# Five attention rows moved into the last batch, own memory for the raw weights, and the nearest-expert step moved

## The chip, the cores and the metric

The kernel runs on one core of one Trainium2 chip. The metric is the device time of one execution in microseconds. Three runs of the kernel before gave 1133.48, 1134.14 and 1136.73 us, so the median is 1134.14 us.

## What is computed

The reference chains three parts, all in float32:

```
p_packed = sm_attn(p, k, v)              # 8 batches x 8 heads, 32 packed queries over 576 keys
out      = sm_attn(q, p_packed, p_packed) # 576 queries over the 32 packed rows
x        = out as 4608 tokens x 512
x        = moe1(x)   # 8 experts, 576 tokens each; experts are filled in the order of sorted logits
x        = moe2(x)   # 8 experts, the best one per token, weighted by its softmax
expert:    relu(x @ w1[e]) @ w2[e]       # 512 -> 1024 -> 512
```

The first mixture has capacity 576 per expert, so which expert closes first has to be found by a search over all logits before the first expert's tokens are known.

## The kernel before

**Attention** (`attention`, L60) loops over 8 batches. Batch `i` makes the packed attention of batch `i` (`pack_scores`, `pack_exp`, `pack_eT`, `pack_v`, `pack_D`, `pack_T`), the query scores of batch `i-1` (`query`), and the softmax and transposes of batch `i-2` (`sm_aT`, `logits`). What comes out per batch is `aT`, the transposed attention weights. An output row tile, called a row below, is `out_rows(b, c)` (L357): two float32 products on TensorE (L367), one copy out of PSUM on ScalarE (L370), one store to the DRAM tensor `xs` from SyncE's queue (L372). There are 8 x 5 = 40 of them in the list `todo`. `fill(n)` takes the next n of them; `FILL` says how many in each batch at three places, `TAIL` how many between the steps that follow the last batch (5, 3, 2, 0).

**Routing.** While the rows that are left run in `forward`, phase 0 of the router runs between them: `nearest` (the best expert per token, seven VectorE instructions) and `search` (eight rounds; each is a comparison `ge` on VectorE, five small products on TensorE at L654, three VectorE instructions down to `cp`, one product, and three or four VectorE instructions from `cmx` to the next `ge`). The search ends with `code`, and `ex`, the chosen expert. Then the token list `idx` is built, and GpSimd gathers the tokens with five indirect DMAs (L1263, into `G`). `nearest` for the first 20 columns of the logits is already done in the last batch: that call is `early()`, with `EARLY = 20`.

**Experts.** A unit is one expert's 576 tokens (units 0 to 7), then blocks of up to 580 tokens of the second mixture. TensorE does the first layer (L1517) and the second (L1572). Each float32 operand is split into a high and a low part, so each product is three. The weights go through four raw buffers of 0.5 MB: a DMA fills one, ScalarE writes the high half (L1460, `w1H`), VectorE the low half (L1466, `w1L`), and then the buffer is free for the next load (`fetch`). Tokens are turned by TensorE (L1300), split by ScalarE (L1301, `XH`) and VectorE (L1302, `XL`). Later phases of the search run between the products of the units.

**Order of the work.** There is no run-time scheduler: each engine runs its own instructions in the order that was written. `Sched` (L1044) keeps a clock per engine while the program is written, and `S.advance` puts instructions of waiting chains (search, splits, token turns) between the rows and products by estimated costs. What becomes ready earlier in that model is written earlier.

**Memory.** The raw buffers come out of a pool that is opened after `closing()` has given the attention's memory back, so they lie where attention tiles lay. Their first load is issued in `fetch`, called from `gather_next` after all rows are written.

## Time and profile before

| | us |
|---|---|
| median of 3 runs | 1134.14 |
| profiled execution, its time | 1134.52 |
| its span | 1132.8 |
| TensorE busy | 1041.8 (92% of the span) |
| VectorE busy | 713.5 (63%) |
| ScalarE busy | 444.6 (39%) |
| GpSimd busy | 488.7 (43%) |

The span is the stretch between the first and the last instruction; 1.7 us lie around it. In the rows below PE is TensorE, PEld its weight loads, DVE VectorE, ACT ScalarE, POOL GpSimd, SP SyncE. Times are counted from the start of the span. A timeline row gives start and duration, then engine, line, operation, output and inputs, and in brackets how long the engine sat idle before and what ended that.

### The profile page before, as it was taken

To read this page: it belongs to the slowest core of one execution; us is meant where nothing else is said; L and a number is where in the kernel's file an instruction comes from. 1 tells how busy PE (TensorE), PEld (TensorE's weight loads), DVE (VectorE), ACT (ScalarE), POOL (GpSimd) and SP (SyncE) were. 2 spreads that over 40 slices of the span, in tenths; PEclk is the share of its full clock that TensorE was granted. 3 is DMA by queue.
4 is the path that set the end of the run, shared out by engine and by line. 5 is a ranking of instruction groups with operands and counts; after the bars stand their busy time and mean duration, and the time that the engine had idled before them with its cause. 6 is when DMAs were issued, how large, how long until landed. Compare 5 with 4: busy or idle time off the path is not lost.

```text
span 1132.8 us, 24490 instructions
## 1 busy us (share of the span) xinstructions
PE 1041.8 (92%) x9152; PEld 967.9 (85%) x9152; DVE 713.5 (63%) x2105; ACT 444.6 (39%) x940; POOL 488.7 (43%) x595
## 2 busy tenths in 40 slices
PE   6689797699899998999999999989999999999996
PEld 4577664588888897989999999979898999999995
DVE  1468777688979889884556566655555556455430
ACT  4467564323332323333434334333443433434331
POOL 1123301212424224047565344477787778742401
PEclk9899899699999999999999999999999999999998
DMA  9989246633243242224345343554445454433301
GB/s 257 278 228 259 53 168 201 158 75 117 64 139 113 80 137 57 99 89 145 117 134 138 99 145 93 135 143 126 126 144 143 106 170 136 127 125 102 99 20 43
DMA packets 117857, 146.90 MB, mean 130 GB/s; under 512 B 55946, under 2 KB 80522, under 8 KB 116704
## 3 DMA queue, kind: packets, MB, share of 16 engines
q1 hardware_dynamic: 102368, 116.43, 35.9%
q0 software_dynamic: 13776, 28.76, 8.7%
q8 instruction: 74, 1.21, 0.5%
q14 instruction: 55, 0.45, 0.2%
q10 hardware_dynamic: 1584, 0.05, 0.1%
HBM read 116.31 MB, written 29.52 MB: 129 GB/s over the span
## 4 chain that ended last, share of the span: by engine, by line
PE 60%; DVE 12%; issue 9%; DMA 9%; POOL 5%; ACT 2%; SPq 2%; POOLq 0%; ACTq 0%; DVEq 0%
PE mm L1572 26%; PE mm L1517 22%; DMA G<-ys,gi 4%; POOL out_dram L1344 3%; PE sc L170 2%; POOL G L1282 2%; PE tr L367 1%; DMA raw<-in_moe_w_dram 1%; PE sc L367 1%; DVE hL L1494 1%; DMA G<-xs,idx 1%; DMA vm<-in_v_dram 1%; PE tr L150 1%; DVE cmx L1008 1%; PE b L150 1%
## 5 line engine op out<-in xcount | busy, mean ns | idle before, releaser
L1517 PE MATMUL mm<-XH,w1H 128*128 128x290 f32 (+3 forms) x1024 | 306.9, 300 | 8.7 <-ACT XH L1301 3.8
L1517 PE MATMUL mm<-XL,w1H 128*128 128x290 f32 (+3 forms) x1024 | 307.9, 301 | 0.5 <-DVE XL L1321 0.3
L1517 PE MATMUL mm<-XH,w1L 128*128 128x290 f32 (+3 forms) x1024 | 305.4, 298 | 2.8 <-DVE w1L L1466 2.7
L1572 PE MATMUL mm<-hH,w2H 128*128 128x288 f32 (+3 forms) x768 | 231.9, 302 | 1.1 <-ACT YT L1577 1.1
L1572 PE MATMUL mm<-hH,w2L 128*128 128x288 f32 (+3 forms) x768 | 232.7, 303 | 0.0
L1572 PE MATMUL mm<-hL,w2H 128*128 128x288 f32 (+3 forms) x768 | 231.7, 302 | 0.1
L1492 ACT ACTIVATE hH<-mm 128x290 fp32r<-128x290 f32 (+3 forms) x256 | 105.7, 413 | 293.4 <-PE mm L1517 279.6
L1517 PEld LDWEIGHTS mm<-XH,w1H 128*128 128x128 f32 x1024 | 195.2, 191 | 11.2 <-ACT XH L1301 4.2
L1517 PEld LDWEIGHTS mm<-XH,w1L 128*128 128x128 f32 x1024 | 195.4, 191 | 3.9 <-DVE w1L L1466 3.5
L1517 PEld LDWEIGHTS mm<-XL,w1H 128*128 128x128 f32 x1024 | 194.7, 190 | 1.6 <-DVE XL L1321 0.8
L1494 DVE SCALAR_TENSOR_TENSOR hL<-mm,hH 128x290 fp32r<-128x290 f32 (+3 forms) x256 | 115.2, 454 | 116.7 <-ACT hH L1492 115.6
L1282 POOL DMA_INDIRECT G<-ys,gi x152 | 158.2, 1041 | 62.8 <-issue 31.7
L1572 PEld LDWEIGHTS mm<-hH,w2H 128*128 128x128 f32 x768 | 144.5, 188 | 1.6 <-ACT YT L1577 1.5
L1572 PEld LDWEIGHTS mm<-hL,w2H 128*128 128x128 f32 x768 | 144.5, 188 | 0.3 <-DVE hL L1494 0.3
L1572 PEld LDWEIGHTS mm<-hH,w2L 128*128 128x128 f32 x768 | 144.4, 188 | 0.1
L1344 POOL DMA_INDIRECT out_dram<-Y,si x93 | 96.1, 1033 | 112.0 <-DVE Y L1542 48.5
L1466 POOL TENSOR_TENSOR w2L<-raw,w2H 128x512 fp32r<-128x512 f32 x48 | 63.2, 1338 | 172.2 <-ACT w2H L1460 172.1
L1577 ACT ACTIVATE YT<-mm 128x288 f32<-128x288 f32 (+2 forms) x96 | 39.9, 419 | 203.8 <-PE mm L1572 202.1
L1308 DVE STREAM_TRANSPOSE XT<-G 128x128 f32<-128x128 f32 x206 | 55.6, 295 | 83.6 <-DMA G<-ys,gi 62.0
L1466 DVE TENSOR_TENSOR w1L<-raw,w1H 128x512 fp32r<-128x512 f32 x128 | 83.8, 677 | 19.6 <-ACT w1H L1460 19.0
L1460 ACT ACTIVATE w1H<-raw 128x512 fp32r<-128x512 f32 x128 | 73.1, 623 | 19.5 <-DMA raw<-in_moe_w_dram 11.5
L1460 ACT ACTIVATE w2H<-raw 128x512 fp32r<-128x512 f32 x128 | 73.1, 622 | 0.0
(383 smaller groups left out, 1544.3 us busy)
## 6 DMA issues: line engine op xcount, KB each, us to landing
raw<-in_moe_w_dram SPq DMA_DIRECT2D x112, 512.0 KB
ys<-Y SPq DMA_DIRECT2D x8, 1152.0 KB
qm<-in_q_dram SPq DMA_DIRECT2D x8, 1024.0 KB
vm<-in_v_dram SPq DMA_DIRECT2D x8, 1024.0 KB
xs<-xm SPq DMA_DIRECT2D x32, 256.0 KB
raw<-in_moe_w_dram SPq DMA_DIRECT2D x64, 128.0 KB
km<-in_k_dram SPq DMA_DIRECT2D x7, 1024.0 KB
G<-ys,gi POOLq DMA_INDIRECT x152
```

The lines of the kernel that those rows point to most:

```text
L150: nc.tensor.transpose(t[:, i, :], src[:, h + i // 2, 128 * (i % 2):128 * (i % 2) + 128], ident)
L170: nc.tensor.matmul(t[32 * c:32 * c + 32, :512].rearrange("p (i j n) -> p j i n", i=2, j=2)[:, j], lhs(h, j), m[:, h], start=True, stop=Tru ...
L1282: nc.gpsimd.indirect_dma_start(out=G[:, g], out_offset=None, in_=ys[:n], in_offset=bass.IndirectOffsetOnAxis(ap=self.gi[:, g:g + 1], axis= ...
L1308: nc.vector.transpose(out=self.x[0][:, :, 32 * g:32 * g + 32], in_=G[:, g].rearrange("p (c i) -> p c i", c=4))
L1344: i = nc.gpsimd.indirect_dma_start(out=to, in_=rows, in_offset=None, out_offset=bass.IndirectOffsetOnAxis(ap=at, axis=0), bounds_check=to. ...
L1460: nc.scalar.activation(a, b, AF.Copy)
L1466: (nc.gpsimd if pool else nc.vector).tensor_tensor(p[0], p[1], p[2], op=OP.subtract)
L1492: nc.scalar.activation(hh, t, AF.Relu)
L1494: ch.ops.append(("vector", 0.37, lambda: nc.vector.scalar_tensor_tensor(hl, t, 0.0, hh.bitcast(F32), op0=OP.max, op1=OP.subtract), ts + 0.2))
L1517: nc.tensor.matmul(t, a[:, c, fs], b[:, c, s], start=(i == 0), stop=(i == 11))
L1572: nc.tensor.matmul(t, l, r, start=(i == 0), stop=(i == 23))
L1577: nc.scalar.activation(YT[:, d, s], t, AF.Copy)
```

## The change

1. `FILL` is used in the last batch only and becomes (0, 1, 1, 3): one row after the exponentials, one after `pack_v`, three ahead of the logits (a new place, `FILL[3]`). So 25 rows are left for `forward` instead of 30.
2. The raw buffers get their own memory, which is never attention memory. The four loads of unit 0's first layer are issued by a hook that runs when the search has chosen the expert (`first_loads`), and `load_rows` is the code of that load, moved out of `fetch`.
3. `early()` moves behind `pack_D` and `sm_aT`.

```diff
-FILL = (0, 0, 0, 0)
+FILL = (0, 1, 1, 3)
...
-        if EARLY and not n1 and EP == 1:
-            early()
         pack_v(i)
-        fill(FILL[2])
+        if not n1:
+            fill(FILL[2])
         pack_D(i)
         if p2 and AT == 0:
             sm_aT(i - 2)
+        if EARLY and not n1 and EP == 1:
+            early()
...
+            if what == "lg" and not n1:
+                fill(FILL[3])
...
+    raws = [raw[:, i] for i in range(4)]
+    queue, landed, due, one_e = [], {}, {}, []
+
+    def load_rows(u, e, c, t):
+        w = m1_w1 if u < E else m2_w1
+        rows = w[bass.ds(e, 1)].rearrange("o (c a i) f -> a c i (o f)", a=4, i=32)[c]
+        for i in range(4):
+            nc.sync.dma_start(t[32 * i:32 * i + 32], rows[i])
+        landed[u, 1, c] = t
+        due[u, 1, c] = S.t["sync"] = max(S.t["sync"], S.t["tensor"] + (2 if u else LAND)) + 2.2
+
+    def first_loads():
+        if one_e or 0 not in P.experts:
+            return
+        one_e.append(nc.values_load(R.ex[0:1, 0:1], engines=[SP], min_val=0, max_val=E - 1))
+        for c in range(4):
+            load_rows(0, one_e[0], c, raws[c])
+
+    P.hooks.append(first_loads)
...
-    raw = wp.tile([128, 4, 1024], F32, name="raw")
-    raws = [raw[:, i] for i in range(4)]
...
-    free = list(raws)
+    free = []
...
+    raw = rp.tile([128, 4, 1024], F32, name="raw")
```

Three places show how the instructions move. First, VectorE in the last batch (`best` to `digits` is the nearest-expert step, `dup` is the scaled packed output that TensorE turns next, `qm<-T` the attention weights that the logits need). Before:

```order
L319 TENSOR_REDUCE mx<-T 128x36
L670 TENSOR_REDUCE best_1874<-LG 128x20
L671 TENSOR_TENSOR rw<-LG,best_1874 128x160
L672 TENSOR_TENSOR rw<-rw,w8b 128x160
L673 TENSOR_REDUCE mxc_1875<-rw 128x20
L675 TENSOR_SCALAR sign<-best_1874 128x20
L677 TENSOR_TENSOR key<-best_1874,sign 128x20
L678 CAST digits_1876<-key 128x4x20
L242 TENSOR_SCALAR dup<-b_66,st 128x128 x2
L338 STREAM_TRANSPOSE qm<-T 128x1152
```

With the change:

```order
L319 TENSOR_REDUCE mx<-T 128x36
L242 TENSOR_SCALAR dup<-b_67,st 128x128 x2
L338 STREAM_TRANSPOSE qm<-T 128x1152
L675 TENSOR_REDUCE best_1930<-LG 128x20
L676 TENSOR_TENSOR rw<-LG,best_1930 128x160
L677 TENSOR_TENSOR rw<-rw,w8b 128x160
L678 TENSOR_REDUCE mxc_1931<-rw 128x20
```

The seven instructions of the step now stand behind `dup` and the transpose.

Second, TensorE in the same place, from the packed output to the query scores of the last but one batch (`bd` times `aT` is a row, `gt` the logits, `wg` the gate, `qT` times `qz` the scores). With the change:

```order
L235 MATMUL b_67<-vr,eT 32x64 x4
L367 MATMUL tr_94<-bd_107,aT 128x256 x2
L150 MATMUL tr_95<-ident,qm 128x128 x4
L150 MATMUL b_66<-ident,qm 128x128 x4
L250 MATMUL b_67<-ident,dup 128x128 x2
L367 MATMUL tr_94<-bd_107,aT 128x256 x2
L367 MATMUL tr_95<-bd_107,aT 128x256 x2
L367 MATMUL b_66<-bd_107,aT 64x256 x2
L284 MATMUL b_67<-qm,gt_111 32x128 x8
L290 MATMUL b_67<-qm,gt_111 32x32 x4
L268 MATMUL tr_94<-wg,qz_102 32x8 x8
L170 MATMUL sc_96<-qT,qz_102 32x2x128 x8
```

Before, the four rows `bd` times `aT` are not there; the fifth stands ahead of the query scores of the batch before.

Third, VectorE ahead of unit 0 (`ge` to the next `ge` is a round of phase 1's search, `w1L` the low halves of the weights). Before:

```order
L1008 TENSOR_TENSOR cp<-two_2113,fold_360 128x120
L1466 TENSOR_TENSOR w1L<-raw,w1H 128x512
L1008 TENSOR_REDUCE cmx<-b_66 128x15
L1008 SCALAR_TENSOR_TENSOR cmx,sel_f<-cmx,f_363 128x15
L1008 TENSOR_SCALAR w<-w,sel_f 128x36
L1008 TENSOR_TENSOR ge<-w,tab 128x15x5x8
L1466 TENSOR_TENSOR w1L<-raw,w1H 128x512
L1008 TENSOR_TENSOR two<-b_66,own 128x64
L1466 TENSOR_TENSOR w1L<-raw,w1H 128x512 x4
L1302 TENSOR_TENSOR XL<-mm_2462,XH 128x4x128
L1302 TENSOR_TENSOR XL<-mm_2463,XH 128x4x128
```

With the change:

```order
L1013 TENSOR_TENSOR cp<-two_2143,fold_361 128x120
L1482 TENSOR_TENSOR w1L<-raw,w1H 128x512
L1013 TENSOR_REDUCE cmx<-b_66 128x15
L1013 SCALAR_TENSOR_TENSOR cmx,sel_f<-cmx,onef 128x15
L1482 TENSOR_TENSOR w1L<-raw,w1H 128x512 x4
L1323 TENSOR_TENSOR XL<-mm_2445,XH 128x4x128
L1323 TENSOR_TENSOR XL<-mm_2446,XH 128x4x128
L1013 TENSOR_SCALAR wt<-w,sel_f 128x36
L1510 SCALAR_TENSOR_TENSOR hL<-mm_2447,hH 128x256
```

Before, `XL` comes in the middle of the fourth round of phase 1, now behind the `cmx` of the second: two of the eight rounds have moved from ahead of unit 0's products to between them. On SyncE the loads still stand behind the stores of all rows, but the first of them no longer carries waits for memory to come free, only the wait of its queue slot.

## Rows read from the trace of the kernel before

**Rows 1.** Page, part 2: granted TensorE clock in 40 slices of 28.3 us, in tenths.
```profile
PEclk9899899699999999999999999999999999999998
```

**Rows 2.** Chain that ended last, 184 to 216 us: start, duration, what.
```profile
189.34 3.44 DMA xs<-xm
...
196.98 6.26 DMA raw<-in_moe_w_dram
...
203.26 6.70 DMA raw<-in_moe_w_dram
...
213.27 2.93 PE mm L1517 x12
```

**Rows 3.** Timeline, 176 to 216 us, all engines.
```profile
180.32 0.32 PE L654 MATMUL b<-oh,ge 128*128 128x64 bf16 x5
...
181.75 2.08 PE L367 MATMUL tr<-bd,vm 128*128 128x256 f32 x8
...
183.35 0.15 DVE L1008 TENSOR_SCALAR ex<-code 128x1 int32<-128x1 f32 x1
...
191.62 0.17 DVE L1008 SCALAR_TENSOR_TENSOR idx<-mt,xr 128x5 int32<-128x5 f32 x1
...
192.92 10.65 SPq L1407 DMA_DIRECT2D raw<-in_moe_w_dram  x16
...
193.69 1.36 POOL L1263 DMA_INDIRECT G<-xs,idx  x1 [49.09 <-DVE oh L1008]
...
195.35 0.96 POOL L1263 DMA_INDIRECT G<-xs,idx  x1 [0.30 <-issue]
...
198.75 0.69 DVE L1466 TENSOR_TENSOR w1L<-raw,w1H 128x512 fp32r<-128x512 f32 x1
...
199.66 0.17 DVE L1008 SCALAR_TENSOR_TENSOR cmx<-cmx,onef 128x15 f32<-128x15 f32 x1
...
206.49 1.94 PE L1300 MATMUL mm<-ident,G 128*128 128x128 f32 x8
...
211.93 1.28 DVE L1302 TENSOR_TENSOR XL<-mm,XH 128x512 fp32r<-128x512 f32 x2
```

**Rows 4.** Waits of TensorE, 124 to 158 us: us in total, times, longest.
```profile
PE tr L250 <- DVE dup L242: 3.0, 1, 3.0
PE sc L170 <- ACT e L194: 1.0, 1, 1.0
```

**Rows 5.** Timeline, 112 to 143 us, the last two batches.
```profile
119.03 2.13 POOL L323 TENSOR_TENSOR T<-T,mx 128x1152 f32<-128x1152 f32 x1 [2.67 <-DVE mx L319]
...
119.47 0.61 DVE L242 TENSOR_SCALAR dup<-b,st 128x128 f32<-128x128 f32 x2 [0.53 <-issue]
...
122.24 0.64 PE L284 MATMUL b<-km,gt 128*32 128x128 f32 x16
...
132.64 2.13 DVE L671 TENSOR_TENSOR rw<-LG,best 128x160 bf16<-128x160 f32 x1
...
134.81 0.24 DVE L672 TENSOR_TENSOR rw<-rw,w8b 128x160 bf16<-128x160 bf16 x1
...
136.34 0.66 PE L250 MATMUL tr<-ident,dup 128*128 128x128 f32 x2 [3.02 <-DVE dup L242]
...
137.79 1.08 PE L284 MATMUL b<-qm,gt 128*32 128x128 f32 x16 [0.79 <-DVE qm L338]
```

**Rows 6.** Windows: busy us (instructions) of PE, PEld, DVE, ACT, POOL, clock, DMA, GB/s.
```profile
138.00:140.00 2.00, 2.00 (x52) 1.79 (x48) 0.78 (x4) 0.00 (x0) 0.00 (x0) 0.50 0.00 0
...
142.00:144.00 2.00, 2.00 (x24) 1.70 (x17) 1.97 (x4) 0.21 (x1) 1.53 (x1) 0.98 0.00 0
194.00:204.00 10.00, 2.74 (x18) 1.73 (x18) 6.11 (x23) 1.80 (x4) 5.00 (x5) 0.50 0.94 220
```

**Rows 7.** Line L1229, 180 to 640 us: the read of the expert on SyncE, min/median/max ns.
```profile
L1229 SPq TENSOR_LOAD <-ex x8: 267/274/1050, 189.8 to 566.1; - x8
```

**Rows 8.** Waits of TensorE, 213 to 1133 us.
```profile
PE b L654 <- DVE ge L1008: 8.0, 7, 2.0
```

More of the change, by code (lines that the diff above doesn't have):

```diff
@@ L416, in attention @@
             drops.extend(middle())
-        fill(FILL[0])
+        if not n1:
+            fill(FILL[0])
         pack_scores(i)
@@ L429, in attention @@
             trans("k", i + 1, j)
-        fill(FILL[1])
+        if not n1:
+            fill(FILL[1])
         if p1:
@@ L448, in attention @@
             sm_sub(i - 1, nc.gpsimd)
-        if EARLY and not n1 and EP == 1:
-            early()
         pack_v(i)
-        fill(FILL[2])
+        if not n1:
+            fill(FILL[2])
         pack_D(i)
@@ L1147, with forward @@
 LCAP = N + -(-IG // 2) * 64
-def forward(tc, ctx, cn, R, R2, wg2, S, P, todo, rows, closing, xs, ys, lst, out, m1_w1, m1_w2, m2_w1, m2_w2):
+def forward(tc, ctx, cn, R, R2, wg2, S, P, raw, todo, rows, closing, xs, ys, lst, out, m1_w1, m1_w2, m2_w1, m2_w2):
     nc = tc.nc
@@ L1196, in forward @@
     gathered, l1_done, lg_done = [0], [-1], [-1]
-    free = list(raws)
-    queue = []
-    landed, due = {}, {}
+    free = []
     class Unit:
@@ L1228, in prepare @@
                 t, i = R2.tb[:, 0], self.u - E
-            self.e = nc.values_load(t[0:1, i:i + 1], engines=[SP], min_val=0, max_val=E - 1)
+            self.e = (nc.values_load(t[0:1, i:i + 1], engines=[SP], min_val=0, max_val=E - 1) if self.u
+                      else one_e[0])
             if not self.one:
@@ L1249, in prepare @@
                     cm.ops.append(("vector", 0.1, lambda: nc.vector.tensor_copy(sa, Ma[:, :, 1]), t))
-            for which in (1, 2):
+            for which in (1, 2) if self.u else (2,):
                 queue.extend((self, which, c) for c in range(4))
@@ L1401, in fetch @@
             w = ((m1_w1, m1_w2) if u.one else (m2_w1, m2_w2))[which - 1]
-            if which == 1 and (not u.u or 2 <= u.u < BYROW):
+            if which == 1 and 2 <= u.u < BYROW:
                 queue.pop(0)
-                t = free.pop(0)
-                rows = w[bass.ds(u.e, 1)].rearrange("o (c a i) f -> a c i (o f)", a=4, i=32)[c]
-                for i in range(4):
-                    nc.sync.dma_start(t[32 * i:32 * i + 32], rows[i])
-                landed[u.u, which, c] = t
-                due[u.u, which, c] = S.t["sync"] = max(S.t["sync"], S.t["tensor"] + (2 if u.u else LAND)) + 2.2
+                load_rows(u.u, u.e, c, free.pop(0))
                 continue
@@ L1721, in tile_attention_moe @@
     P.add(0)
-    forward(tc, ctx, cn, R, R2, wg2, S, P, todo, rows, attn.close, xs, ys, lst, out, m1_w1, m1_w2, m2_w1, m2_w2)
+    forward(tc, ctx, cn, R, R2, wg2, S, P, raw, todo, rows, attn.close, xs, ys, lst, out, m1_w1, m1_w2, m2_w1, m2_w2)
 _INS = ["q", "k", "v", "p", "moe_w_gate", "moe_w1", "moe_w2", "moe2_modality_id", "moe2_w_gate", "moe2_modality_bias",
```

## The prediction

> **What bounds the kernel now.** I read the page first: over 40 slices the granted TensorE clock is near full but for one slice, the eighth (198 to 227 us), where it is 6 tenths [rows 1]. So there is one hole. The chain of waits through that hole says what TensorE waits for [rows 2]: the last store of an attention row, 3.44 us, then the weight loads, the last of which takes 6.70 us and lands at 209.96; 3.3 us later, at 213.27, unit 0's products run without a stop. The timeline of that stretch shows the rest [rows 3]: the search has named the expert at 183.35, yet the first load of its weights is issued at 192.92, 9.6 us later, since the buffer lies in attention memory and so waits for the last store. Then I looked for holes ahead of it with the waits of TensorE in the last batch [rows 4], and found 3.0 us for `dup` and 1.0 us for the exponentials.
>
> **1. The nearest-expert step.** It stands ahead of `dup` on VectorE. Its multiply-compare `rw` takes 2.13 us, as long as the subtraction on GpSimd beside which it runs; the next step of the same shape takes 0.24 [rows 5]. TensorE sits idle for 3.02 us until `dup` is there [rows 5]. With the change `dup` comes first. It may meet the same GpSimd subtraction, but in the batch before it did so and took 0.61 for both halves [rows 5], so I take it as not held. The step itself then runs behind the transpose `qm`, when that subtraction is over, and nothing on TensorE waits for it until the search.
>
> **2. Five rows.** A row costs TensorE 1.04 us (two in 2.08 [rows 3]), five cost 5.2. One goes into the 1.0 us wait for the exponentials [rows 4]. Four (4.2) go where TensorE now waits 3.0 for `dup` and 0.8 for `qm` [rows 5]. So TensorE reaches the logits some 0.4 us later than at 137.79. Against that stands the clock: behind the 3 us hole it is 0.50 in 138 to 140, and 0.98 in 142 to 144 [rows 6]; the logits' first products take 1.08 there and took 0.64 in the batch before [rows 5]. From 137.8 to about 142 the work would take some 2.1 us less at the full clock. How much of that comes through? VectorE is busy 1.97 of 2.0 us behind the scores [rows 6], so the chain is largely its own. I take 0.7 us earlier for all that follows; the bounds are 2.1 earlier (all of it) and 1.1 later (one row is not covered and the clock gives nothing). The five copies on ScalarE and the five stores lie beside this; if a copy is late, it is the bank of the next logits that waits, for the same 1.0.
>
> **3. 25 rows beside the search.** The eight rounds keep the rows between them, so the expert is named at 183.35 - 0.7 = 182.6. The rows end with the two that now end at 183.83 [rows 3], so at 183.1. The last store is issued at about 184.3 (the copy and the issue lie between) and lands at about 187.8 by the 3.44 of rows 2. Five rows' stores and copies leave the stretch in which the loads are issued.
>
> **4. The loads.** On SyncE they still stand behind every store. The read of the expert takes 0.27 to 1.05 us [rows 7], so the first load goes out at about 185.5 instead of 192.92. Sixteen took 10.65 us [rows 3], including waits for their eight slots: the last is issued at 196.2 and lands 3.44 (a transfer with little beside it) to 6.70 us later [rows 2], so between 199.6 and 202.9. By bytes: 2.1 MB at the 220 GB/s of the stretch [rows 6] are 9.5 us, so 195; that is no limit here.
>
> **5. The gather.** It waits for the token list and for the last store. The list is there at 191.8 [rows 3], 1 us before the store has landed, and GpSimd starts 0.9 us behind the store. Now the list comes last: at 191.1, and the gather starts at about 192.0. The second of the five (1.36 + 0.3 + 0.96 us [rows 3]) is issued at 194.6 and lands at 198.1 to 201.3. The first two are what unit 0 needs to begin.
> The clock bears on this step: the few products that build the list stand at its end, and with the rows gone at 183.1 TensorE is nearly idle ahead of them. Before, the clock was at 0.50 in 194 to 204 [rows 6], behind the last row, whose store is issued at 189.34 [rows 2]. If it falls as much earlier, those products, under 1 us in all, run at half speed, and the list is up to 0.9 us later. The Trainium skill, TensorE: Matmul & The Clock Gate, section What's actually happening, has it that the throttled clock is the default and only activity lifts it, which would make it so; by that rule the sum below is 1127.4 at most, by the row it is 1126.5.
>
> **6. VectorE ahead of unit 0.** Its order sets the start. Phase 1's second `cmx` ends at 199.83 [rows 3]; 0.7 earlier, and four low halves at 0.69 [rows 3] are now put in front of it, mostly into waits: I add 0.6, so 199.7. Behind it come four more low halves (2.8) and `XL` (1.28 [rows 3]): 203.8. If the loads land last, at 202.9, the same 3.3 us as in rows 2 end at 206.2; if the gather does, at 201.3, the second half of the turn (1.94 for both [rows 3]), its copy and `XL` end at about 204.2. I take 204.0, near VectorE's own chain, as both transfers are mostly in front of it: 9.3 us before 213.27.
>
> **7. What is paid back.** Two rounds of phase 1 no longer run in the hole but between unit 0's products. A round's counting products cost TensorE 0.32 at the full clock [rows 3], the product behind them about as much: 1.3 for two rounds if nothing hides it, 0.6 if half does; I take 0.9. And a round makes TensorE wait when VectorE is late: 8.0 us in 7 waits over the rest of the kernel [rows 8], 1.1 each; I add 0.4, with 0 and two such waits (2.2) as bounds. Taken together: 1.3 (0.6 to 3.5). The choice of expert 1 comes later against unit 0's start by two rounds, and its weights and tokens too. Before, TensorE waited for gathered tokens between units for 2.0 us in 4 waits [rows 8]; I cost a change there at nothing, since the work of unit 0's second layer covers it, and have the lack of that cover as part of a rival.
>
> **Sum.** The profiled execution took 1134.52 us, 0.4 above the median of the runs. 1134.52 - 9.3 + 1.3 = 1126.5. All after unit 0's start is filled by TensorE, so the gain stays.
>
> **Rivals.**
> *The transfers end last.* Weights and gather now run side by side from 192 on, with the second layer's loads right behind. Speaks for it: with the gather beside them a load took 6.70, and the stretch moved 220 GB/s at a DMA share of 0.94 [rows 2, 6]. Against: half of the weights have landed by 192. Then unit 0 starts at 206.2 to 207, and the time is 1134.52 - 6.7 + 1.3 = 1129.1. The Trainium skill, DMA: Bandwidth & Descriptors, section Issuing engines are not separate DMA queues, says that transfers of all issuing engines run on the same 16 engines and interleave, which is this rival's mechanism.
> *The loads are not early.* They share SyncE's queue and its slots with the stores. If the first goes out only when the last store has landed (187.8), the sixteenth is issued at 198.5 and lands at up to 205.2; unit 0 starts at 208.5: 1134.52 - 4.8 + 1.3 = 1131.0. Against it: all but the last few stores have landed by then.
> *Slower: the search stalls TensorE inside unit 0.* Six rounds of phase 1 are left when unit 0 starts, now with `w1L`, `XL` and `hL` of the unit ahead of them on VectorE, and TensorE's products stand behind each round's count. The longest such wait was 2.0 us [rows 8]. Six of 2.0 give 1134.52 - 9.3 + 1.3 + 12 = 1138.5. It decides from 1.3 us per round on (no gain left), and makes the kernel slower by over 0.3% from 1.9 on. Against it: only 7 waits of 1.1 us in all phases before. Weights of unit 1 that come late would show as one wait in the same place, of up to what the order leaves uncovered.
>
> **How the numbers follow.** The forecast has 0.62, transfers last 0.18, loads not early 0.08, stalls in the search 0.06; 0.06 is left for shifts that I don't see, two thirds of it near no change. A change of 0.3% (3.4 us, so below 1130.7) is about what a measurement of this kernel can tell from none. The first two cases are faster: 0.80. Same 0.12, slower 0.08. For the range: at the low end the last batch gives 1.4 more, the paid back part is 0.6, and unit 0 starts 1 us earlier: 1123.4; at the high end the transfers and 3.5 paid back: 1131.3. I take 1122.8 to 1131.3.
>
> **What would show it.** In the profile after: no wait of TensorE for `dup` and the clock full up to the scores (step 1 and 2); the expert named within 1 us of 182.6 (step 3); the first weight load at about 185.5 and the gather at about 192 (4, 5); the first uninterrupted products of unit 0 at 204, behind `XL` on VectorE and not behind a transfer (6). The forecast is wrong if the expert is named after 184, if unit 0 starts after 206, or if TensorE waits over 4 us more between there and the end.

## The result, and the profile after

The changed kernel took 1123.01 us (median of 4 runs, 1122.01 to 1124.33), the kernel before 1133.85 in the same comparison (4 runs, 1133.48 to 1136.73). The ratio is 0.9876, 95% interval 0.9845 to 0.9907: 10.5 to 17.6 us faster, with 14.1 in the middle. The two medians by themselves lie 10.8 us apart, at the near edge of that interval. The forecast, 7.6 us (a ratio of 0.993), lies outside it: the sign was right, the size too small. The forecast's range ended at 11.3 us faster (1122.8 us): the median lies just inside that end, the middle of the interval beyond it. The profiled execution took 1122.01 us, its span is 1120.3.

The page shows the hole between 198 and 227 us half closed: the eighth slice of the clock (196 to 224 us here) is 8 tenths instead of 6 [rows 1].

```profile
PEclk9889998899999999999999999999998999999998
```

In the last batch the waits of [rows 4] are gone: of TensorE's waits for `dup` and for the exponentials no row is left between 124 and 158 us. The timeline of the stretch (start, duration, engine, line) has what answers to [rows 5]:

```profile
119.10 0.61 DVE L242 TENSOR_SCALAR dup<-b,st 128x128 f32<-128x128 f32 x2
...
132.04 0.61 DVE L242 TENSOR_SCALAR dup<-b,st 128x128 f32<-128x128 f32 x2
...
134.17 0.33 DVE L676 TENSOR_TENSOR rw<-LG,best 128x160 bf16<-128x160 f32 x1
...
136.73 0.64 PE L284 MATMUL b<-qm,gt 128*32 128x128 f32 x16
...
137.62 0.32 DVE L298 STREAM_TRANSPOSE lgw<-b 128x128 f32<-128x128 f32 x1 [1.96 <-PE b L290]
...
139.51 1.13 PE L367 MATMUL tr<-bd,aT 128*128 128x256 f32 x4
...
143.52 1.43 DVE L511 TENSOR_TENSOR T<-T,mx 128x576 f32<-128x576 f32 x2
...
144.32 0.59 ACT L370 ACTIVATE xm<-tr 64x512 f32<-64x512 f32 x1 [0.41 <-PE tr L367]
...
144.94 1.26 ACT L512 ACTIVATE T<-T 128x576 f32<-128x576 f32 x2
...
146.23 1.35 DVE L516 TENSOR_REDUCE mx<-T 128x36 f32<-128x1152 f32 x1
...
152.68 0.28 DVE L1013 TENSOR_REDUCE best<-LG 128x16 f32<-128x128 f32 x1
```

`rw` takes 0.33 us instead of 2.13, `dup` comes 3.4 us earlier against the `dup` of the batch before (12.94 us behind it instead of 16.38), and the logits' first products take 0.64 instead of 1.08. The last five rows, from L511 on, are the tail of the last batch: the subtraction on VectorE, a row copy `xm` and the last batch's exponential on ScalarE, the row sums `mx` that VectorE takes of the exponentials, and `best`, with which the nearest-expert step of the last 16 columns begins; that row is called the start of the search below. `lgw` (L298) is VectorE's first row behind the logits' products, and L367 the first row products of the tail on TensorE. The same rows in the kernel before (its timeline, 138 to 156 us):

```profile
139.13 0.32 DVE L298 STREAM_TRANSPOSE lgw<-b 128x128 f32<-128x128 f32 x1 [1.40 <-PE b L290]
...
142.62 2.00 PE L367 MATMUL tr<-bd,aT 128*128 128x256 f32 x8
...
145.04 1.43 DVE L506 TENSOR_TENSOR T<-T,mx 128x576 f32<-128x576 f32 x2
...
147.39 0.59 ACT L370 ACTIVATE xm<-tr 64x512 f32<-64x512 f32 x1 [0.41 <-PE tr L367]
147.88 1.24 ACT L507 ACTIVATE T<-T 128x576 f32<-128x576 f32 x2
...
149.16 1.35 DVE L511 TENSOR_REDUCE mx<-T 128x36 f32<-128x1152 f32 x1 [1.40 <-ACT T L507]
...
155.60 0.28 DVE L1008 TENSOR_REDUCE best<-LG 128x16 f32<-128x128 f32 x1
```

There the exponential starts 2.84 us behind the subtraction that feeds it, right behind the fifth row copy `xm`; in the changed kernel 1.42 us, again right behind that copy, which now ends at 144.91. So VectorE, which waited 1.40 us for the exponentials before, does not wait for them any more. The search starts 2.9 us earlier.

From the naming of the expert to unit 0, the timeline of the changed kernel (compare [rows 3]):

```profile
178.84 2.08 PE L367 MATMUL tr<-bd,km 128*128 128x256 f32 x8
...
180.44 0.15 DVE L1013 TENSOR_SCALAR ex<-code 128x1 int32<-128x1 f32 x1
...
183.73 8.97 SPq L1179 DMA_DIRECT2D raw<-in_moe_w_dram  x16
...
188.12 0.17 DVE L1013 SCALAR_TENSOR_TENSOR idx<-mt,xr 128x5 int32<-128x5 f32 x1
...
189.26 1.16 POOL L1284 DMA_INDIRECT G<-xs,idx  x1 [46.18 <-DMA raw<-in_moe_w_dram]
...
198.68 1.15 ACT L1476 ACTIVATE w1H<-raw 128x512 fp32r<-128x512 f32 x2 [2.79 <-DMA raw<-in_moe_w_dram]
...
200.56 1.28 DVE L1323 TENSOR_TENSOR XL<-mm,XH 128x512 fp32r<-128x512 f32 x2
...
201.89 0.58 PE L1533 MATMUL mm<-XL,w1H 128*128 128x256 f32 x1 [0.24 <-DVE XL L1323]
```

The rows now end together with the search (180.92 and 180.44). The last to arrive is the fourth weight buffer: ScalarE waits 2.79 us for it, at 198.68; the chain of waits has the load itself, answering to the 6.70 of [rows 2]:

```profile
192.39 6.19 DMA raw<-in_moe_w_dram
```

Behind it stand `w1H`, `w1L`, `XL` and, at 201.89, the products that run without a stop, 11.4 us before the 213.27 of [rows 2]. The windows that answer to [rows 6] (busy us of the engines, then clock, DMA share, GB/s):

```profile
138.00:140.00 2.00, 2.00 (x45) 1.83 (x37) 1.89 (x5) 0.95 (x4) 0.00 (x0) 1.00 0.87 288
194.00:204.00 10.00, 5.99 (x26) 4.59 (x27) 6.24 (x15) 4.42 (x8) 3.24 (x4) 0.50 1.03 295
```

The clock is full in the last batch; ahead of unit 0 it is 0.50, the lower of its two levels (1.2 GHz), until unit 0 has begun.

### The profile page after: what moved, and what is told of

Read it like the earlier page. It is cut to its first block, busy times and chain, and to the rows that moved or that the text cites. A ratio compares the mean times of both kernels' runs of the same rounds, so it can differ in the third digit from the quotient of the medians.

```text
span 1120.3 us, 24491 instructions
## 1 busy us (share of the span) xinstructions
PE 1042.0 (93%) x9152; PEld 967.5 (86%) x9152; DVE 708.0 (63%) x2105; ACT 443.8 (40%) x940; POOL 487.8 (44%) x595
## 4 chain that ended last, share of the span: by engine, by line
PE 66%; DVE 12%; issue 7%; DMA 6%; POOL 4%; SPq 2%; ACT 1%; POOLq 0%; DVEq 0%; ACTq 0%
PE mm L1588 28%; PE mm L1533 26%; DMA G<-ys,gi 2%; PE sc L170 2%; POOL G L1303 2%; POOL out_dram L1365 2%; PE tr L367 1%; DVE hL L1510 1%; DMA vm<-in_v_dram 1%; PE tr L150 1%; DMA G<-xs,idx 1%; PE b L150 1%; PE sc L367 1%; PE b L659 1%; PE mm L1321 1%
## 6 DMA issues: line engine op xcount, KB each, us to landing
vm<-in_v_dram SPq DMA_DIRECT2D x8, 1024.0 KB, 10.6
```

## Experiments

**How the profiles are compared.** The `dup` of the last batch but one lies ahead of everything that was changed, and stands anywhere from 115.9 to 121.4 us in the profiles. So the stages are counted from its start, in us; "search" is the row `best` above, "product" unit 0's first one at the first layer's line, "first load" the first on SyncE.

| kernel | logits | search | expert named | first load | gather | product |
|---|---|---|---|---|---|---|
| before | 18.32 | 36.13 | 63.88 | 73.45 | 74.22 | 92.76 |
| changed | 17.63 | 33.58 | 61.34 | 64.63 | 70.16 | 81.75 |
| step_only | 14.89 | 32.23 | 59.96 | 69.56 | 70.33 | 89.27 |
| fill_only | 20.13 | 36.07 | 63.80 | 67.42 | 72.60 | 85.71 |
| step_fill | 17.63 | 33.57 | 61.30 | 64.91 | 70.09 | 81.84 |
| loads_only | 18.30 | 36.81 | 64.54 | 71.02 | 83.77 | 92.94 |
| loads_late | 18.33 | 36.54 | 64.28 | 72.37 | 74.72 | 92.09 |
| before_tail | 18.31 | 36.73 | 64.48 | 74.33 | 75.10 | 93.98 |
| rows3 | 15.76 | 32.82 | 60.57 | 65.89 | 69.88 | 86.97 |
| after_gland | 17.63 | 33.57 | 61.34 | 64.62 | 70.16 | 82.94 |
| after_again | 17.63 | 33.57 | 61.33 | 64.61 | 70.13 | 80.96 |
| hold_w2 | 17.64 | 33.58 | 61.32 | 64.61 | 70.13 | 81.93 |
| hold_two | 17.63 | 33.58 | 61.33 | 64.62 | 70.13 | 79.35 |
| hold_two_warm | 17.64 | 33.58 | 61.33 | 64.61 | 70.14 | 80.81 |
| gland_low | 17.63 | 33.58 | 61.33 | 64.61 | 70.13 | 81.46 |
| two_warm | 17.63 | 33.58 | 61.31 | 64.60 | 70.11 | 80.41 |
| after_third | 17.62 | 33.57 | 61.31 | 64.59 | 70.11 | 81.70 |

Kernels whose program is the same up to the search agree there within 0.02 us (the changed kernel's kin) or 0.7 (before, loads_only and loads_late). The three profiles of the changed kernel itself (changed, after_again, after_third) agree at the product within 0.8. Steps smaller than that are not told from chance below.

### The parts alone (4 kernels, one chip, before 1136.86 us)

**step_only.**

```diff
-        if EARLY and not n1 and EP == 1:
-            early()
         pack_v(i)
...
             sm_aT(i - 2)
+        if EARLY and not n1 and EP == 1:
+            early()
```

> The kernel before, with the nearest-expert step alone moved behind the transposed probabilities (no rows in the last batch, loads as before). Theory A (the wait for dup is what the step costs: TensorE stood idle for 3.02 us behind it): dup comes some 2 us earlier (the length of rw, 2.13), the logits start about 2 us earlier, but the last batch's five row copies still stand ahead of the exponential on ScalarE, at the same distance behind the logits; the search starts about 2 us earlier and the whole time falls by about 2 us. Theory B (my prediction: behind the scores VectorE's own chain rules, so that only a part comes through): 0 to 0.7 us. In both the wait for dup is at most 1 us.

Measured: 1133.46 us, ratio 0.9962 (0.9941 to 0.9983), 1.9 to 6.7 us faster. VectorE's timeline:

```profile
120.75 0.61 DVE L242 TENSOR_SCALAR dup<-b,st 128x128 f32<-128x128 f32 x2 [0.53 <-issue]
133.69 0.61 DVE L242 TENSOR_SCALAR dup<-b,st 128x128 f32<-128x128 f32 x2
...
152.98 0.28 DVE L1008 TENSOR_REDUCE best<-LG 128x16 f32<-128x128 f32 x1
```

The search starts 3.9 us earlier than before (32.23 against 36.13), the product 3.5. All by which `dup` came earlier (3.44) comes through, and more, as VectorE waits only 0.7 us for the exponentials instead of 1.40: theory A, which had 2, was nearer than the forecast's 0.7, and both were low.

**fill_only.**

```diff
-FILL = (0, 0, 0, 0)
+FILL = (0, 1, 1, 3)
```

with the calls of `fill` that go with it, as in the change.

> The kernel before, with the five rows alone (one, one and three of them in the last batch; the nearest-expert step and the loads as before). Theory A (the dup wait is the step's): two rows lie in the two waits ahead of dup and cover 2 of 4 us, three more lie behind dup and are not covered, apart from 0.8 us; the logits come 1 to 2 us later, at the full clock, which gives back up to 2.1: the expert is named within 1 us of 183.35, five rows fewer stand beside the search, the whole time is 0 to 1 us longer or shorter. A rival: the rows' copies and stores, which lie earlier, let the last store land earlier, so that the loads go out up to 2 us earlier: then the time falls by up to 2 us though the search starts no earlier.

Measured: 1127.77 us, ratio 0.9926 (0.9900 to 0.9952). The search starts where it did (36.07 against 36.13), yet the product comes 7.05 us earlier, more than any of the theories had. The timeline shows where from:

```profile
185.72 9.29 SPq L1412 DMA_DIRECT2D raw<-in_moe_w_dram  x16
...
190.90 1.19 POOL L1268 DMA_INDIRECT G<-xs,idx  x1 [46.12 <-DMA raw<-in_moe_w_dram]
```

The five rows no longer stand behind the search, so their last store lands earlier: the loads go out 6.0 us earlier (67.42 against 73.45), though their buffers still lie in attention memory. The gather, which now waits for the token list, starts only 1.6 us earlier. So the loads are 5.2 us ahead of it instead of 0.8, and from the gather's start to the product it takes 13.1 us instead of 18.5. These 5.4 and the 1.6 are the gain.

**step_fill.** Both of these edits, the loads as before.

> The kernel before with the step moved and the five rows, loads as before. In the changed kernel the expert is named 2.9 us earlier than before; this run should show the same 2.9 us (180.4), as the loads come later in the program. If the last store still ends the wait of the loads, they go out 2.9 us earlier or so and the time falls by about 3 us; if what rules the start of unit 0 is the rows' last store, and the five rows have left the stretch, by up to 5 us. My prediction would have had 0.7 us here. With the loads alone giving the rest, the three parts add up to 11 to 12 us.

Measured: 1122.93 us, ratio 0.9872 (0.9837 to 0.9906): all of the changed kernel's gain, without its load edit. Stage by stage it equals the changed kernel; the first load goes out 0.3 us later, the product comes at 81.84 instead of 81.75. The ratio of the changed kernel, 0.9876, is from another comparison.

**loads_only.** The changed kernel with `FILL` back at zeros and `early()` back in its old place.

> The kernel before with weight buffers of their own and the loads right behind the choice of the expert; no rows in the last batch and the step in its old place. The expert is named at 183.35 as before. Theory A (the last batch gave 2.9 of the 12.5 us in the profiles): unit 0 starts about 8.5 us earlier than before, and the time falls by about 8 us. Rival: with five more rows beside the search, two to three more remain behind it, and their copies and stores stand ahead of the loads on the same queue: the first load goes out 2 to 3 us later after the choice than in the changed kernel (3.3 us there), and the time falls by only 5 to 6 us.

Measured: 1134.95 us, ratio 0.9995 (0.9969 to 1.0021): no gain that can be told. The timeline of its hole:

```profile
188.99 8.91 SPq L1179 DMA_DIRECT2D raw<-in_moe_w_dram  x16
198.00 0.46 SPq L372 DMA_DIRECT2D xs<-xm  x1
200.93 4.26 ACT L1476 ACTIVATE w1H<-raw 128x512 fp32r<-128x512 f32 x8 [12.45 <-DMA xs<-xm]
...
201.74 1.58 POOL L1284 DMA_INDIRECT G<-xs,idx  x1 [58.66 <-ACT w1H L1476]
```

The hook put the sixteen loads ahead of the last row's store on SyncE. That store is issued at 198.00 (`w1H`, whose output lies where attention tiles lay, waits 12.45 us for it) and lands 2.83 us later, and the gather, which reads the stored rows, starts 0.9 us behind the landing, as it did before: 9.5 us later than before, counted from that `dup` (83.77 against 74.22). The profile names `w1H` as what released it, which ended in between. The rival named the place, the stores on the same queue, but the other way round: the loads are ahead, and what they gained is lost again.

So of the 11.0 us by which the product is earlier, the step alone gave 3.5 and the rows alone 7.05, together 10.5, and the loads nothing that can be told, neither alone nor on top: with the rows gone by the time the expert is named, attention memory is free almost as early as the loads can use it (first load at 64.91 in step_fill, 64.63 in the changed kernel).

### Where the pieces come from (4 kernels, before 1367.64 us)

In these runs and in all that follow TensorE was granted a lower clock, whatever the kernel: 0.88 to 0.91 in the mean of an execution, instead of 0.97 to 0.98 above. So their medians, 1339 to 1368 us, compare only with the kernel before beside them. The last batch of the changed kernel runs at 1.00 here too, and the stages up to the product agree with the others', as the table shows. Behind unit 0's first layer they do not: unit 1 of the unaltered changed kernel starts 150.1 us behind that `dup` instead of 147.8. One page row (after_again), lowest from some 500 us on:

```profile
PEclk9899979999999997989699897697896879699989
```

**loads_late.**

```diff
-    P.hooks.append(first_loads)
...
     closing()
+    S.until(lambda: 0 in P.experts)
+    first_loads()
```

on loads_only, so that the loads stand behind all stores.

> The run with the early loads alone, but with the sixteen loads behind all the rows' stores on SyncE, still into memory of their own. In the run with the loads alone, unit 0's first product stood 92.94 us behind the dup of the batch before the last (92.76 in the kernel before), since one store stood behind the loads and the gather waited for it. Theory A (the store in the way took back what the early loads gave; all that own buffers can give is the landing of the last store): the first load goes out within 2 us of the last store, about 2 us earlier than before, the gather as before, and the first product is 1 to 2.5 us earlier than before (90.3 to 91.8 behind that dup). Rival (own buffers are worth the 7 us of my forecast as soon as nothing takes them back): 85 to 87. The whole time falls by 0 to 3 us (A) or by 6 to 8 (rival).

Measured: the loads go out 1.1 us earlier than before, the product comes 0.7 us earlier (92.09), no more than the spread between profiles. Own buffers are not worth the rival's 7 us, and not shown to be worth A's 1 to 2.5: the loads are only 2.35 us ahead of the gather. The ratio, 0.9927 (0.9880 to 0.9975), is lower than the 0.7 us explain, and no higher than that of rows3 beside it, whose product comes 5 us earlier still; so the whole times of this comparison settle nothing about the start of unit 0, and what the kernel gains behind it is open.

**before_tail.**

```diff
-TAIL = (5, 3, 2, 0)
+TAIL = (0, 8, 2, 0)
```

on the kernel before.

> The kernel before, with the five rows that stand ahead of the last batch's exponential moved behind it (the first two numbers of TAIL from 5 and 3 to 0 and 8). Theory A (the exponential is late because five row copies stand ahead of it on ScalarE: 2.84 us behind the subtraction's start before, 1.42 in the changed kernel): it starts 1.4 us behind the subtraction, the search about 1.4 us earlier (34.7 us behind the dup of the batch before the last, instead of 36.13); the rows run a little later and take it back on TensorE where the softmax waits, so the whole time changes by less than 1.5 us. Theory B (VectorE's own chain rules behind the scores): the search starts within 0.3 us of 36.13.

Measured: ratio 1.0037 (0.9999 to 1.0074). The timeline:

```profile
143.37 1.43 DVE L506 TENSOR_TENSOR T<-T,mx 128x576 f32<-128x576 f32 x2
...
144.22 1.29 ACT L507 ACTIVATE T<-T 128x576 f32<-128x576 f32 x2 [8.24 <-DVE T L506]
...
152.73 0.32 DVE L298 STREAM_TRANSPOSE lgw<-tr 128x128 f32<-128x128 f32 x1 [1.97 <-PE tr L290]
...
154.54 0.28 DVE L1008 TENSOR_REDUCE best<-LG 128x16 f32<-128x128 f32 x1
```

The exponential now starts 0.85 us behind the subtraction and 2.0 us earlier than before, and the search still no earlier (36.73 against 36.13). VectorE's wait of 1.40 us for the exponentials is gone, as theory A had it. But all eight rows now stand ahead of the last batch's logits on TensorE, and VectorE waits 1.97 us for those instead. So neither theory holds as written: VectorE's own work from `lgw` to the search is 15.05 to 15.10 us in before, in step_only, in fill_only, in the changed kernel and here alike, and what comes on top is its wait: 1.40 in before, 0.69 in step_only, none in fill_only and the changed kernel, 1.97 here. In the changed kernel the wait goes without another in its place, since the rows themselves come earlier: they start 20.41 us behind that `dup` instead of 23.15, since the logits come 0.69 earlier and the scores behind them run at the full clock.

**rows3.**

```diff
-FILL = (0, 1, 1, 3)
+FILL = (0, 1, 1, 1)
```

> The changed kernel with three rows moved ahead instead of five (one, one and one). If the rows beside the search set the last store and a row is worth 1.04 us there, the rows end 2.1 us later against the search's start than in the changed kernel. Theory A (rows and search end together with five, so that two rows fewer let the rows end last again): the logits come 1.5 to 2 us earlier, the search 0.5 to 1.3 us earlier, the rows end some 2 us behind the expert's naming; with the loads and the gather behind the stores the first product is 0 to 1 us later than in the changed kernel (81.75 us behind the dup of the batch before the last). Rival (the rows never mattered, the early loads did): the first product is 0.5 to 1.3 us earlier, as the search.

Measured: ratio 0.9933 (0.9888 to 0.9979). The search starts 0.76 us earlier and the rows end 2.5 us behind the naming, as A had it, but the product comes 5.2 us later than in the changed kernel, where A had at most 1:

```profile
185.39 10.03 SPq L1179 DMA_DIRECT2D raw<-in_moe_w_dram  x16
...
189.38 1.20 POOL L1284 DMA_INDIRECT G<-xs,idx  x1 [47.74 <-DMA raw<-in_moe_w_dram]
...
204.30 1.15 ACT L1476 ACTIVATE w1H<-raw 128x512 fp32r<-128x512 f32 x2 [4.49 <-DMA raw<-in_moe_w_dram]
```

The loads lead the gather by 4.0 us only, and the fourth buffer is there at 204.30, 18.9 us behind the first load; in the changed kernel 15.0. With five rows instead of three the lead over the gather is 5.5 us instead of 4.0; that it is the lead that counts is argued from this and the rows of other kernels (last section), not shown by itself.

**after_gland.**

```diff
-GLAND = 8.5
+GLAND = 12.0
```

> The changed kernel with the planner's time for the two first turns of unit 0 moved from 8.5 to 12 us behind the gather, so that about one more round of the next search runs ahead of unit 0 and one fewer between its products. Theory A (the end ahead of unit 0 is the last weight load, not VectorE): the round hides beside the transfers, unit 0 starts at most 0.7 us later, and with one wait fewer in unit 0 the time is 0 to 1 us shorter. Rival (VectorE's chain rules there, as my prediction had it): unit 0 starts about 3 us later (one round took 3.3 us there) and the time is 1.5 to 3 us longer.

Measured: ratio 0.9919 (0.9877 to 0.9962). The product comes 1.2 us later than in the first profile of the changed kernel and 2.0 later than in after_again: more than A's 0.7, less than the rival's 3. Four rounds of the next search run ahead of unit 0, as before the change, and four in its first layer, instead of two and six. Yet that layer, from its first product to the first of the second layer, takes 34.0 us (32.2 to 32.7 in the three profiles of the changed kernel): fewer rounds in it did not make it shorter.

### The transfers and the clock ahead of unit 0 (4 kernels, before 1356.01 us)

**after_again.** The changed kernel, unaltered.

> The changed kernel once more, unaltered, on the chip of the three runs beside it. Its time against the kernel before: a ratio of 0.9845 to 0.9907, as in the first comparison. By the normalised stages (unit 0's first product 11.0 us earlier) and nothing paid back behind it, 11 us or 0.990; with the 1.3 us of my forecast paid back 0.9915; with 1 to 3 us more gained behind it, as two of three pairs of profiles have it, 0.987 to 0.989.

Measured: ratio 0.9898 (0.9861 to 0.9936), which holds the first comparison's 0.9876; the product comes at 80.96.

**hold_w2.**

```diff
+    hold = [True]
+    tiny = sp.tile([128, 4], F32, name="tiny")
     def fetch():
         while queue and free:
             u, which, c = queue[0]
+            if hold[0] and which == 2:
+                return
...
+    nc.vector.tensor_copy(tiny, raw[:, :, 0])
+    hold[0] = False
+    fetch()
     for i in range(E + need):
```

The splits of the held-back weights move from products 0, 4, 8 and 12 of unit 0's first layer to 4, 7, 10 and 13.

> The changed kernel with unit 0's four second-layer loads held back until the second turn's XL (a read of raw's first column behind XL on VectorE frees their buffers), and their splits moved from products 0, 4, 8, 12 to 4, 7, 10, 13. Theory C (the transfers rule the start: from 192 us on the DMA engines are busy all the time, and second-layer loads that go out at 192.96 take part of it from the last weight load and the gather): the last first-layer load lands about 2 to 3 us earlier than 198.58 and the first product comes 1.5 to 3 us earlier than 81.75 us behind the dup of the batch before the last (79 to 80.3). Theory B (my prediction: VectorE's own chain rules the start): no earlier than 81.3. If the later second-layer weights are not there at product 4, 7, 10 or 13, TensorE waits in unit 0 and the time gives it back.

Measured: ratio 0.9911 (0.9876 to 0.9946), product at 81.93. The fourth buffer is no earlier:

```profile
199.23 1.15 ACT L1481 ACTIVATE w1H<-raw 128x512 fp32r<-128x512 f32 x2 [2.62 <-DMA raw<-in_moe_w_dram]
```

That is 79.76 us behind that `dup`, 79.58 in the changed kernel. The second-layer loads, which now go out at 202.59 instead of 192.96, were not what delays it, and theory C falls in this half. The first layer of unit 0 then took 35.6 us, about 3 us longer.

**hold_two.**

```diff
-            nc.sync.dma_start(t[32 * i:32 * i + 32], rows[i])
+            (nc.scalar if both and i % 2 else nc.sync).dma_start(t[32 * i:32 * i + 32], rows[i])
```

on hold_w2, with the expert's number read on both engines.

> As the run before, and the sixteen first-layer loads are issued from two engines, SyncE and ScalarE, eight each. In the runs so far the distance from the gather's start to unit 0's first product goes with the lead that the loads have over the gather: 18.5 to 18.9 us at a lead of 0.8, 17.4 at 2.3, 17.1 at 4.0, 11.6 to 13.1 at 5.2 to 5.5. Theory C: with the issues of sixteen loads in about 4.5 us instead of 9, nearly all of them are ahead of the gather, and the first product comes another 1 to 2.5 us earlier (77 to 79 behind that dup); then the gather and its turn end last. Rival (by bytes the 2.1 MB take as long whichever engine issues them): within 0.5 us of the run with the second layer held back alone.

Measured: ratio 0.9898 (0.9862 to 0.9933), product at 79.35, 2.6 us earlier than hold_w2:

```profile
195.12 1.15 ACT L1481 ACTIVATE w1H<-raw 128x512 fp32r<-128x512 f32 x2 [0.47 <-issue]
...
200.60 0.58 PE L1539 MATMUL mm<-XL,w1H 128*128 128x256 f32 x1 [0.83 <-DVE XL L1323]
```

ScalarE waits for no transfer at the fourth buffer any more (75.50 behind that `dup`, over 4 us earlier), and VectorE's low halves and `XL` end last, so that the gain is 2.6 and not 4: theory C's other half. It does not last: with the second layer's loads held back the first layer takes 37.4 us, and unit 1 starts at 150.9, no earlier than in after_again (150.1). The DMA issues of the two queues:

```profile
182.36 4.84 ACTq L1179 DMA_DIRECT2D raw<-in_moe_w_dram  x8
...
184.24 7.72 SPq L1179 DMA_DIRECT2D raw<-in_moe_w_dram  x8
```

ScalarE's eight start 1.9 us before SyncE's, which stand behind the last rows' stores, and are all out 2.5 us ahead of the gather (189.75). The Trainium skill, DMA: Bandwidth & Descriptors, section Issuing engines are not separate DMA queues, has it that a second issuing engine saves only the time of issuing, usually small. Here issuing is not small, 9.0 us for the sixteen on one engine, and the measurement decides: over 4 us at the fourth buffer. Part of that is ScalarE's earlier start, which no run separates from the issuing.

**hold_two_warm and two_warm.**

```diff
+    def warm(n):
+        mms.append(mms.pop(0))
+        for _ in range(n):
+            nc.tensor.transpose(mms[-1][:, :128], cn["ident"], cn["ident"])
     for i in range(2):
+        warm((6, 2)[i])
         units[0].turn_rows(i)
+    warm(5)
```

two_warm leaves the second-layer loads as in the changed kernel; it was run later, beside after_third, the changed kernel unaltered (before 1356.39 us).

> As the run before, with thirteen transposes of the identity that nobody reads on TensorE around the two turns (six, two and five), so that TensorE is busy for some 3 us more ahead of unit 0. In the changed kernel the granted clock is 0.50 from 188 to 204, up to some 3 us behind unit 0's first product. Theory D: the clock is full earlier, and unit 0's products reach the full speed up to 2.5 us earlier, of which half comes through: the second layer of unit 0 starts about 1 us earlier than in the run without them. Rival: the transposes push the turns back, or the clock stays at its lower level until the products themselves have run for as long as before; then 0, or up to 1 us lost.

> The changed kernel with the sixteen loads on two engines' queues and the thirteen transposes of the identity around the two turns; the second-layer loads of unit 0 as in the changed kernel. In the run that held them back as well, the clock was full from 198 us on, unit 0's 34th product ended 2.9 us earlier than in the changed kernel, but the first layer of unit 0 then took 1.5 to 3 us longer. Without holding them back: the 34th product again 2 to 3 us earlier than in the changed kernel, the first layer 29 to 31 us long from its first product, and the whole time 2 to 3 us under that of the changed kernel. If the second-layer loads then take the transfers away from the first layer (the reason for holding them back), 1 us or less.

> The changed kernel, unaltered, as the measure for the two runs beside it on the same chip: 0.9845 to 0.9936 of the time of the kernel before, by the two comparisons so far.

Measured: hold_two_warm 0.9882 (0.9838 to 0.9926), two_warm 0.9873 (0.9846 to 0.9901), after_third 0.9879 (0.9846 to 0.9913). Windows of after_third, then of two_warm:

```profile
202.00:204.00 2.00, 2.00 (x11) 2.00 (x11) 0.33 (x1) 0.71 (x2) 2.00 (x2) 0.50 0.95 350
```

```profile
202.00:204.00 2.00, 1.78 (x14) 1.57 (x14) 1.67 (x2) 0.78 (x3) 1.66 (x2) 1.00 1.02 370
```

With the thirteen transposes that nobody reads ahead of it, unit 0 starts at the full clock. two_warm's first layer takes 30.4 us (32.5 in after_third) and its unit 1 starts 3.4 us earlier, 146.6 against 150.0 behind that `dup`. In the whole time this does not show: the two intervals lie on each other, so it is ahead at unit 1 and not shown to beat the changed kernel. hold_two_warm's first layer takes 34.2 us: holding the loads back costs 3.8 of them.

**gland_low** (same comparison).

```diff
-GLAND = 8.5
+GLAND = 5.5
```

> The changed kernel with the planner's time for the two first turns 5.5 instead of 8.5 us behind the gather: the turns stand ahead of the second count of phase 1's third round on, so one round fewer has been counted when unit 0 begins. By my prediction's step 7 a round more between unit 0's products costs 0.6 to 3.5 / 2, some 0.3 to 1.8 us, of the first layer of unit 0 (32.2 to 32.7 us in the runs of the changed kernel on the first two chips), and VectorE's chain would let the first product start up to 3 us earlier. By the reading after the runs (the transfers set the first product; in the first layer only waits count, and where the rounds' lists fall decides them) the first product is within 0.7 us of 81 to 81.8 behind the dup of the batch before the last, and the first layer takes between 32 and 34 us.

Measured: ratio 0.9964 (0.9937 to 0.9990), against 0.9879 beside it. The product comes where it did (81.46), but the first layer takes 34.9 us, and in it (TensorE's waits, 200.1 to 235 us)

```profile
PE b L659 <- DVE ge L1013: 3.1, 2, 1.6
```

instead of 0.7 in after_third: these 2.4 us are the whole difference of the first layer. No round has moved into that layer (six in both); they stand elsewhere in it, and the next expert is named 3.3 us later. Most of the 2.4 is made up by the start of unit 1 (0.3 us behind after_third). The loss comes later: 5.0 us by the start of unit 4, 11.2 by that of unit 5, against 10.6 between the medians. Why the later units lose so much was not followed. So the time at the product and that of the first layer do not tell the whole time.

## Why the forecast was too small

**Steps 1 and 2, last batch: the step that failed.** The forecast had 0.7 us earlier for all that follows, with 2.1 as the bound; it was 2.9 in the profiles, 2.55 counted from the same `dup` (the rest, 0.37, lies ahead of the change and is luck of the two profiles). Two terms were mis-sized.

First, the logits were to come 0.4 us later and came 0.69 earlier (17.63 against 18.32): moving the step gained 3.43 there (step_only), not the 3.02 that TensorE waited, and five rows cost 2.74 (step_only to the changed kernel), so that 2.5 of their 5.2 were covered.

Second, the clock. It did save what step 2 had, some 2.1 us: from the logits to the first row of the tail TensorE took 2.78 us instead of 4.83. The forecast let only about half of that through, since "VectorE is busy 1.97 of 2.0 us behind the scores, so the chain is largely its own". That was right of the 2 us looked at, and not of the stretch behind them, where VectorE waits 1.40 us for exponentials that stand behind five row copies on ScalarE; the sum had that wait at nothing. With the scores at the full clock the rows and their copies come 2.7 us earlier, and the wait is gone. So 0.69 from the logits, 0.45 from their faster products (`lgw` comes 0.89 us behind their start instead of 1.34) and 1.40 from the wait make up the 2.55.

**Step 3** held: the expert is named 27.76 us behind the search's start (27.75 before), the rows end 0.5 behind the naming, as forecast.

**Steps 4 to 6** held in their sum: from the naming to the uninterrupted products the forecast had 21.4 us (182.6 to 204.0), the profile has 21.45 (180.44 to 201.89). First load 3.3 us behind the naming (2.9 forecast), fourth buffer landed 14.9 behind the first load (14.1 to 17.4). But not what ends last: it is the transfer (the fourth buffer, 198.58), the mechanism of the first rival, and not VectorE, whose `XL` stands behind it. That the sum fits to 0.1 us is therefore in part luck. And the price was put at the wrong edit: the text gave the gain to the early loads, while fill_only and loads_only show that the moved rows bring it. Its own numbers held the hint, the rows' last store landing at 187.8 instead of 192.8 [rows 2].

**Step 7 had the wrong sign.** 1.3 us were to be paid back behind unit 0's start; in the profiles 1.1 more were gained (213.27 to 1132.8 is 919.5 us, 201.89 to 1120.3 is 918.4). Two rounds more do run inside unit 0's first layer, six counts instead of four, as the forecast had it, but the layer takes 32.2 us instead of 34.3, since the waits there shrink. TensorE's waits in that layer before:

```profile
PE b L654 <- DVE ge L1008: 1.3, 1, 1.3
PE b L1008 <- DVE AB L1008: 0.9, 1, 0.9
```

and after:

```profile
PE b L659 <- DVE ge L1013: 0.4, 1, 0.4
```

The making of expert 1's list (`AB`) has moved out of the layer. That this is chance of the arrangement and no rule, gland_low (six rounds, 34.9 us) and after_gland (four, 34.0) show. Nor is it the first layer that left the 1.1: the lead over the kernel before, 11.0 us at the product, is 12.2 at unit 1, 9.2 at unit 2, 13.8 at unit 4 and 12.1 at the end. What makes it go up and down was not followed. Over the whole rest the waits for `ge` are as before, 8.3 us in 8 against [rows 8]:

```profile
PE b L659 <- DVE ge L1013: 8.3, 8, 1.7
```

Steps 2 and 7 make up the difference: 2.2 us (2.9 less 0.7) and 2.4 (1.1 and 1.3), together 4.6, stand against the 4.5 between 1126.5 and the profile's 1122.0. Of these, step 2 is accounted for and step 7 is not.

**The rivals.** "The transfers end last" had the mechanism right and the time wrong, as steps 2 and 7 gave more than it lost. "The loads are not early" did not happen (3.3 us behind the naming; it had 5.2), but early they were by the rows and not by the load edit. "The search stalls TensorE" did not happen in this arrangement; gland_low has longer waits for `ge`, 3.1 us in the first layer, far from the 12 that the rival needed.

## What to carry to other kernels

Before a gain is given to one edit of several, ask of each edit alone what it makes free and when: here the rows set the last store, the store set the loads, and the edit that was named for the loads moved nothing. A busy share holds for the stretch that it was read from: VectorE was 98% busy in one window and waited 1.40 us a little later. Follow the engine's waits to the end of the chain, and ask what comes last when one of them goes, as before_tail did. When loads are put earlier on a queue, look at what is now behind them, since one store behind sixteen loads cost all that they had gained here.

## What the runs showed of the hardware

- The distance from the gather's start to unit 0's first product goes with the lead of the first load over the gather, and not evenly: 18.5 us at a lead of 0.8 (before), 17.4 at 2.35 (loads_late), 17.1 at 4.0 (rows3), 13.1 and 11.75 at 5.2 (fill_only, step_fill), 11.6 at 5.5 (the changed kernel). Between 196 and 204 us the DMA engines are busy all the time in rows3 as in the changed kernel, but move 217 GB/s in the one and 308 in the other. Why 1.2 us of lead decide over 4 us was not settled; in the changed kernel the second layer's loads do not delay the fourth buffer, as hold_w2 shows; they were not held back in rows3.
- TensorE, kept busy with 13 transposes that nobody reads, was granted 1.00 instead of 0.50 when unit 0 began, and a product of 256 columns took 0.28 us instead of 0.41. The Trainium skill, TensorE: Matmul & The Clock Gate, section What's actually happening, says that the lower level is the default and activity lifts it; the trace agrees.
- The kernel before took 1134 to 1137 us (medians) in two comparisons and 1356 to 1368 in three, with a mean granted clock of 0.97 and 0.89. The longer times are on record for three chips, numbers 13, 3 and 11, and number 3 stands beside one of the shorter ones as well, so they are not shown to be a property of a chip; the cause is open. Stages up to unit 0's first product could be compared across them, whole times could not.
